# A schedule builder's clock learns of GpSimd's hold on VectorE's port: new order table, and batch 0's row copies by either engine

## The chip, the cores and the metric

The kernel runs on one core of one Trainium2 chip. The core has five engines with a queue each: TensorE (PE, with its weight loads PEld), VectorE (DVE), ScalarE (ACT), GpSimd (POOL) and SyncE (SP), which here only issues DMAs. Each engine takes its instructions in the order of the program. The metric is the device time of one execution in microseconds (us), as the median of several runs.

## The reference

Nystrom attention over 8 batches of 8 heads, 576 rows, 64 columns, and then a block with a layer norm and two dense layers:

```python
q_lm = q.reshape(B, H, 32, 18, D).mean(axis=3)       # 32 landmarks; k_lm likewise
A, Bm, C = sm(q, k_lm), sm(q_lm, k_lm), sm(q_lm, k)  # softmax(a @ b.T / 8)
Z = Bm.T / (norm1(Bm) * norminf(Bm) + 1e-06)
for _ in range(6):
    Z = 2 * Z - Z @ Bm @ Z
x = A @ Z @ C @ v                     # then heads side by side: 8 x 576 x 512
xn = (x - mu) / sqrt(var + 1e-06) * g_ln
out = x + maximum(xn @ w_ch1, 0) @ w_ch2             # 512 -> 2048 -> 512
```

## The kernel before

**Work.** Batches go through three stages. *Attention* (`attention0` for batch 0, `attention2` for the groups (1), (2), (3, 4), (5, 6), (7)): landmarks, the exponentials (`ec` of the k side, `ea` of the q side, by ScalarE's Exp out of the matmuls `psec` and `psea`), the softmax and six iterations of the 32 x 32 inverse (`st`; batch 2 and 7 do them as whole 128 x 128 matrices). The softmax of a batch is a chain on VectorE: `rsum`, `rcr`, `st`, `bmT`, a masked `st`, which TensorE then needs for the gram matrix. *First layer* (`first_layer`): hidden chunks `hT` of 128, each four matmuls into `psh` and a Relu. Since x itself is a product of `ea` and a small matrix, the layer multiplies the weights with the small matrix first (`m`). *Second layer* (`second_layer`): row blocks of 128, 16 matmuls `bank<-w,hT` each; from batch 4 on by seven products of half matrices (`seven_products`), for which VectorE mixes halves of `hT` and GpSimd those of `w2`. At its end VectorE adds x (`xblk`), scaled by `rstd`.

**Side work.** The rows of x (`xblk`) come from two matmuls per block of 128 rows (`rows_of`, `two_rows`, `part_of_rows`), copied out of PSUM. VectorE takes each block's statistics (`six`, `stats`: the MEASURE steps); when all of the batch `current[0]` are there, ScalarE makes `lnv` and `rstd` (`deviations`). The weights of the first layer are centered in place by VectorE in eight steps (`center_w1`, rows `w<-w,less`, two 128 x 512 pieces each). GpSimd casts the loaded q, k and v to fp16 (rows `nat<-stg`, `natv<-stg`; ScalarE may take a cast of q or k if GpSimd is behind); VectorE turns and adds them up for the landmarks (`xT`, `sT`, `part`: the JOB steps; a matmul and ScalarE's copy `lm` follow, the "spread").

**Order.** While the program is built, `run` draws the next piece from five streams, numbered 0 attention, 1 totals, 2 first layers, 3 rows of batch 0, 4 second layers, the first one that is ready by the builder's own clock (`Clock`), and between them `help_out` puts in side work, numbered 5 JOB, 6 MEASURE, 7 CENTER, 8 MIX, 9 MIX_W2, 10 CAST, 11 LOAD. `Clock.note` keeps, for every instruction noted, when its engine will be free (`free`) by a table of costs (`took`). The order of noting is the order in each engine's queue, and it is fixed once the program is built: the clock is not on the chip. MEASURE, CENTER and JOB are drawn only if

```python
if clock.free["DVE"] <= now + lead():     # 0.7 us once batch 1 is ready, 0.4 before
```

`sooner(n, at)` gives a copy to ScalarE (190 + 0.79 n ns by the builder's costs) or to VectorE (140 + 1.15 n), whichever it expects to be done first.

`AFTER` is a table of holds: `(0, 17): (4, 31)` says that stream 0 does not take its step of index 17 until stream 4 has taken 31 steps. In the kernel before, the second layer of batch 1 begins with step 53 of stream 4 (it sets `current[0]` to 1); attention step 20 (the 21st) is batch 2's first with `psec`. JOB steps 8 to 17 are batch 2's. The clock knows that a centering (`locks`) and a GpSimd instruction keep each other waiting when the GpSimd instruction has been noted already.

Of the kernel before, what the change touches and what calls it, by code (L numbers as in the profile page):

```python
# [16 lines left out]
P = 128  # L17
# [3 lines left out]
def kernel(  # L21
# [63 lines left out]
    class Clock:  # L85
# [74 lines left out]
        def note(self, i):  # L160
# [26 lines left out]
            if type(i).__name__ == "InstDMACopy":  # L187
                start = max(self.free[e], ready)
                self.free[e] = start + (580 if e == "SP" else 100)
                half_ = size[0][0] <= 64 and any(n.startswith("stg") for n in writes)  # L190
                self.wire = (max(start + 1650, self.wire)
                             + count[0] * size[0][0] * 4 / (150.0 if half_ else 385.0))
                self.loads = self.loads[-24:] + [(start, self.wire)]
                self.issued += 1
                late_ = 1500 if self.issued <= 4 else 600 + min(2200, 0.8 * (self.wire - start - 1650))
                done = self.wire + late_
                start = done
            elif e == "PE":
                cols = count[0]
                if self.count == self.mark - self.LEAD:  # L200
                    self.ahead = self.now()
                if self.count == self.mark:
                    self.mark += self.BLOCK
                    ready = max(ready, self.fetched)
                    asked = max(self.ahead, self.fetched - 200)
                    behind = max([w for t, w in self.loads if t <= asked] + [0.0])
                    self.fetched = max(asked + 1200, behind + 400) + 2450
                self.count += 1
                rows_, cols_ = tuple(i.tile_size)
                self.cells.append((self.now(), cols / 2.4 * rows_ * cols_ / 128 ** 2))  # L210
                if tuple(i.tile_size) == (128, 128):
                    if self.small:
                        self.free[e] = max(list(self.lanes.values()) + [self.free[e]]) + 100
                        self.small, self.lanes = False, {}
                    start = max(self.free[e], ready)
                    self.free[e] = start + max(cols / (1.2 if start < 5200 else 2.4) + 3, 56)
                    done = self.free[e] + 160
                else:
                    if not self.small:
                        self.small, self.lanes = True, {}  # L220
                        self.free[e] += 95
                    elif self.shape != (rows_, cols_):
                        self.free[e] = max(list(self.lanes.values()) + [self.free[e]]) + 85
                    self.shape = rows_, cols_
                    lane = [(a, c) for a in range(i.tile_position[0], i.tile_position[0] + rows_, 32)
                            for c in range(i.tile_position[1], i.tile_position[1] + cols_, 32)]
                    start = max([self.free[e], ready] + [self.lanes.get(x, 0.0) for x in lane])
                    self.lanes.update((x, start + max(cols / 2.4 + (19 if cols == 288 else 0), 30)) for x in lane)
                    self.free[e] = start + (8 if rows_ == 64 and cols < 128 else 4)
                    done = self.lanes[lane[0]] + 160  # L230
            else:
                start = max(self.free[e], ready)
                if e == "Pool":
                    for a, z in self.locks:
                        if a <= start < z:
                            start = z
                self.ready = start
                done = start + self.took(i, e, count[0], max(count[1:] + [0]))
                self.free[e] = done - self.OVERLAP[e]
                if e == "Pool":  # L240
                    self.pool = self.pool[-8:] + [(start, done)]
                if e == 'DVE' and count[0] == 1024 and writes[0] in parted_w1:
                    self.locks = self.locks[-4:] + [(start, done)]
            for n in reads:
# [620 lines left out]
                block_done(j)  # L865
        return copies

    def one_row(b):
        ea, zcbd = row_zc[b]
        j, at = row_blocks[b].pop(0)  # L870
        xb = x_of(j)
        psy = banks.take([P, 512])
        for u in range(U):
            MM(psy[:, ts(u, 4 * D)], ea[u][:, ds(at, P)], zcbd[u][:].rearrange("p h d -> p (h d)"))
        sooner(512, clock.at(psy))(xb[:], psy)
        block_done(j)

    def part_ready(b):
        return max(banks.next(2), 0.0 if row_part[b][0] in x_blk else xpool.next("xblk"))

# [11 lines left out]
    def rows_of(bs, ea, zcbd):  # L892
        for i, b in enumerate(bs):
            t0 = 0
            while t0 < S:
# [9 lines left out]
                for u in range(U):  # L905
                    MM(psy[:, ts(u, 4 * D)], ea[U * i + u][:, ds(at, P)],
                       zcbd[U * i + u][:].rearrange("p h d -> p (h d)"))
                (sooner(512, clock.at(psy)) if b else scalar.copy)(
                    xb[rows, :], psy[rows if n == P else ds(side, n), :])
                t0 += n  # L910
                if pb + n == P:
# [269 lines left out]
    def attention2(bs, c):  # L1181
# [152 lines left out]
                in1=heads_of[w % 2][:, :, None].broadcast_to([P, 4, D]),  # L1334
                op=ALU.mult)
        ready.update(bs)
        yield from (rows_later if bs[0] >= LATER else rows_of)(bs, ea, zcbd_buf[z0:z0 + W])

    stats_of, rstds = {}, {}

# [73 lines left out]
    class First:  # L1414
# [10 lines left out]
        def two_products_of_heads(self, f):  # L1425

            t = ps2.tile([P, 2, 512], FP32, name="psm", tag="p2")
            one = self.products(f, [banks.take([P, 512]), t[:, 0, :]])
            two = self.products(f + 1, [banks.take([P, 512]), t[:, 1, :]])
            copies = two_rows(self.b) if 2 * f in PAIRS and self.b >= LATER else lambda: None  # L1430
            self.copies(f, one)
            self.copies(f + 1, two)
            copies()
# [43 lines left out]
    def first_layer(b):  # L1477
# [3 lines left out]
            return  # L1481
        two = b >= 1
        if two:
            yield lambda: max(banks.next(2), ps2.next("p2", 2 if 0 in PAIRS and b >= LATER else 1), mprod.next("m16", 2), clock.at(l1.zt),
                              rows_ready(b) if 0 in PAIRS and b >= LATER else 0.0)
            l1.two_products_of_heads(0)
        else:
            yield lambda: max(banks.next(2), mprod.next("m16"), clock.at(l1.zt))
            l1.product_of_heads(0)
        for m in range(MCH):  # L1490
            yield lambda: max(ps2.next("p2"), clock.at(l1.m16[m // 4], *l1.ea),
                              part_ready(b) if m == PART[b % 2] and b in row_part else 0.0,
                              max(banks.next(2), xpool.next("xblk")) if m in ONES and b >= LATER else 0.0)
            l1.chunk(m)
            if m == PART[b % 2] and b in row_part:
                part_of_rows(b)
            if m in ONES and b >= LATER:
                one_row(b)
            if b in row_zc and not row_blocks[b] and b not in row_part:
                row_zc.pop(b)  # L1500
            chunks[b] = m + 1
# [3 lines left out]
                yield lambda: max(banks.next(2), mprod.next("m16"))  # L1505
                l1.product_of_heads(m // 4 + 1)
            if two and m == 4:
                yield lambda: max(banks.next(2), ps2.next("p2", 2 if 4 in PAIRS and b >= LATER else 1), mprod.next("m16", 2),
                                  rows_ready(b) if 4 in PAIRS and b >= LATER else 0.0)
                l1.two_products_of_heads(2)  # L1510
        for t in l1.ea:
            aexp.unpin(t)
        if b in (0, 1, 2, 4, 6, 7):
            asm.unpin(l1.zt)

    chunks, PART, PAIRS, ONES = {}, (8, 6), (0,4), ()
    LATER = 5

    def first_layer0(l1):
        l1.product_of_heads(0)  # L1520
# [239 lines left out]
    def help_out(hurry=False):  # L1760
# [66 lines left out]
    begun_first = [0]  # L1827

    AFTER = {
        (0, 17): (4, 31), (0, 23): (4, 75), (0, 34): (2, 51), (0, 53): (4, 171),  # L1830
        (0, 64): (4, 200), (0, 66): (2, 77), (0, 99): (4, 461), (0, 104): (4, 521),
        (0, 105): (4, 524), (0, 110): (4, 550), (1, 5): (4, 90), (2, 26): (0, 2),
        (2, 34): (4, 23), (2, 47): (4, 96), (2, 53): (4, 106), (2, 66): (4, 187),
        (2, 74): (4, 199), (2, 87): (4, 224), (2, 88): (4, 236), (2, 94): (4, 258),
        (2, 98): (4, 276), (2, 104): (4, 305), (2, 105): (4, 306), (2, 110): (4, 349),
        (2, 112): (4, 392), (2, 138): (4, 475), (2, 160): (4, 648), (3, 3): (2, 27),
        (4, 3): (0, 3), (4, 11): (2, 29), (4, 122): (0, 40), (4, 133): (0, 42), (4, 172): (0, 56),
        (4, 174): (0, 57), (4, 237): (2, 87), (4, 241): (2, 91), (4, 333): (2, 110),
        (4, 407): (2, 121), (4, 438): (2, 126), (4, 592): (2, 147), (4, 595): (2, 147),
        (4, 601): (2, 150), (4, 602): (2, 148), (4, 623): (2, 153), (5, 18): (4, 96),  # L1840
        (5, 26): (4, 119), (5, 30): (2, 66), (5, 43): (0, 53), (5, 49): (0, 65),
        (5, 62): (4, 265), (5, 64): (4, 281), (6, 5): (2, 43), (6, 15): (4, 208),
        (6, 34): (4, 640), (7, 5): (4, 88), (8, 1): (4, 290), (8, 7): (4, 559), (9, 4): (4, 231),
        (9, 9): (2, 93), (9, 14): (0, 80), (9, 15): (4, 257), (9, 16): (4, 279), (10, 5): (2, 46),
        (10, 10): (4, 71), (10, 20): (0, 43), (10, 30): (4, 196), (10, 34): (0, 84),
    }
    taken = [0] * 12
    JOB, MEASURE, CENTER, MIX, MIX_W2, CAST, LOAD = range(5, 12)
# [137 lines left out]
```

## Time and profile before

| | |
|---|---|
| runs | 263.0, 263.37, 263.76 us; median 263.37 us |
| profiled execution | 264.7 us, span 263.0 us, TensorE's clock granted in full |
| busy time | PE 252.0, DVE 209.7, ACT 171.5, POOL 137.3 us |
| HBM | 36.7 MB read, 9.4 MB written |

The span runs from the first instruction to the last. A row of the trace in order of time gives the start, the length, the engine, the line of the program (the helpers' lines L309 and L315 for nearly all), the operation, what it writes and reads by the program's names, shapes, how many were merged, and in brackets the idle time of the engine before it and what ended that. Rows of stretches give, for each engine, the busy time and in parentheses the number of instructions. A row of the waits gives who waited for whom: total us, times, longest.

### The profile page before, as it was taken

The page shows a single profiled execution, that of the slowest core. Times are in us where ns is not written, and L with a number is a line of the kernel's source. Part 1 is how long each engine was busy: PE and PEld are TensorE (multiplying, and loading weights), DVE is VectorE, ACT ScalarE, POOL GpSimd, SP SyncE. Part 2 cuts the span into 40 slices and gives each one's busy share as a digit, 9 for nine tenths or more (in the row PEclk, how much of TensorE's full clock was granted, in tenths as well). Part 3 has the DMA queues.
Part 4 walks back from the last instruction along what each step waited for, and adds up shares of the span by engine and source line. Part 5 has one row for each costly group of instructions (what it writes and reads, how often), then busy time and mean ns, then how long its engine had stood idle before and what let it go on. Part 6 is the DMA issues. An engine that isn't in the chain of part 4 may idle for free.

```text
span 263.0 us, 8556 instructions
## 1 busy us (share of the span) xinstructions
PE 252.0 (96%) x3519; PEld 167.8 (64%) x3519; DVE 209.7 (80%) x475; ACT 171.5 (65%) x335; POOL 137.3 (52%) x163
## 2 busy tenths in 40 slices
PE   7799889999799999999999999999999999999994
PEld 6645654556355574456655556688877875888883
DVE  2677774999979998989898967788389899696862
ACT  2588797548675887678987767655877854775000
POOL 5287779999962869989999938300000005000000
PEclk9999999999999999999999999999999999999999
DMA  6999999999957898779813011110240006100705
GB/s 241 377 396 377 378 392 386 354 267 318 358 159 207 234 374 294 191 185 298 270 53 82 7 40 40 42 40 4 53 109 2 4 16 156 32 2 0 161 16 185
DMA packets 24126, 46.68 MB, mean 178 GB/s; under 512 B 2964, under 2 KB 3224, under 8 KB 24088
## 3 DMA queue, kind: packets, MB, share of 16 engines
q1 hardware_dynamic: 23608, 45.50, 54.5%
q10 hardware_dynamic: 480, 0.66, 0.7%
q8 instruction: 27, 0.44, 0.7%
q14 instruction: 11, 0.09, 0.1%
HBM read 36.70 MB, written 9.44 MB: 175 GB/s over the span
## 4 chain that ended last, share of the span: by engine, by line
PE 75%; DVE 10%; DMA 8%; ACT 3%; issue 1%; POOL 1%; SPq 0%; ACTq 0%; DVEq 0%
PE bank L315 49%; PE psh L315 19%; DMA wstg<-in_moe_w_ch_dram 6%; DVE m L309 2%; DMA stg<-in_k_dram 2%; DVE w L309 2%; PE pscv L315 2%; PE psd L315 2%; ACT xblk L309 1%; DVE six L309 1%; PE psea L315 1%; DVE xblk L309 1%; DVE part L309 1%; ACT hT L309 1%; PE psec L315 1%
## 5 line engine op out<-in xcount | busy, mean ns | idle before, releaser
L315 PE MATMUL bank<-w,hT 128*128 128x512 f16 (+3 forms) x528 | 110.0, 335 | 0.0
L309 ACT ACTIVATE hT<-psh 128x576 f16<-128x576 f32 x122 | 75.9, 653 | 22.5 <-PE psh L315 21.1
L315 PEld LDWEIGHTS <-hT 128*128 128x128 f16 x656 | 60.2, 98 | 30.5 <-issue 5.0
L315 PE MATMUL psh<-ea,m 128*128 128x288 f16 x512 | 78.5, 286 | 1.0 <-ACT ec L309 0.9
L315 PEld LDWEIGHTS <-m 128*128 128x128 f16 x512 | 49.4, 98 | 19.7 <-issue 2.3
L309 DVE SCALAR_TENSOR_TENSOR xblk<-bank,rstd,xblk 128x256 f32<-128x256 f32 (+2 forms) x77 | 39.1, 542 | 15.6 <-PE bank L315 15.3
L309 POOL TENSOR_TENSOR ea<-ea,lns 128x576 f16<-128x576 f16 x14 | 18.0, 1298 | 54.0 <-ACT lns L309 54.0
L309 POOL CAST nat<-stg 128x1152 f16<-128x1152 f32 x24 | 28.9, 1223 | 9.8 <-DMA stg<-in_v_dram 4.7
L309 DVE BATCH_NORM_STATS2 six<-xblk 128x6 f32<-128x512 f32 x36 | 24.3, 675 | 2.1 <-ACT xblk L309 1.9
L309 POOL CAST natv<-stg 128x1152 f16<-128x1152 f32 (+1 forms) x17 | 19.3, 1161 | 7.8 <-DMA stg<-in_v_dram 7.8
L309 DVE STREAM_TRANSPOSE xT<-nat 128x576 uint32<-128x576 uint32 x28 | 21.4, 762 | 0.0
L309 DVE SCALAR_TENSOR_TENSOR st<-st,bank 128x128 f16<-128x128 f16 (+3 forms) x36 | 13.2, 365 | 6.6 <-PE bank L315 6.4
L315 PE MATMUL bank<-w2mix 128*128 128x256 f16 x128 | 17.3, 273 | 0.0
L315 PE MATMUL bank<-w2mix,hT 128*128 128x256 f16 x128 | 16.9, 273 | 0.0
L309 ACT COPY xblk<-bank 128x512 f32<-128x512 f32 (+1 forms) x21 | 12.4, 594 | 5.9 <-PE bank L315 5.8
L309 ACT ACTIVATE lns<-psd 128x576 f32<-128x576 f32 x16 | 10.3, 643 | 7.9 <-PE psd L315 7.6
L309 DVE TENSOR_REDUCE part<-xT 128x32 f16<-128x576 f16 x20 | 14.4, 741 | 0.2
L315 PEld LDWEIGHTS <-st 32*32 32x32 f16 (+1 forms) x380 | 7.0, 90 | 11.3 <-DVE st L309 6.2
L315 PEld LDWEIGHTS <-w2mix 128*128 128x128 f16 x128 | 12.4, 98 | 1.9
L309 ACT ACTIVATE ec<-psec 128x256 f16<-128x256 f32 (+1 forms) x42 | 11.9, 424 | 2.3 <-PE psec L315 2.0
L309 POOL TENSOR_TENSOR asum<-asum 128x256 f32<-128x256 f32 (+1 forms) x20 | 12.4, 621 | 1.6
L309 ACT CAST m<-bank 128x512 f16<-128x512 f32 x16 | 9.3, 589 | 5.8 <-PE bank L315 5.8
(133 smaller groups left out, 374.4 us busy)
## 6 DMA issues: line engine op xcount, KB each, us to landing
stg<-in_q_dram SPq DMA_DIRECT2D x16, 576.0 KB, 6.4
stg<-in_k_dram SPq DMA_DIRECT2D x16, 576.0 KB, 5.9
out_dram<-xblk SPq DMA_DIRECT2D x66, 128.0 KB, 2.4
wstg<-in_moe_w_ch_dram SPq DMA_DIRECT2D x16, 512.0 KB, 7.3
stg<-in_v_dram SPq DMA_DIRECT2D x5, 576.0 KB, 7.6
stg<-in_v_dram SPq DMA_DIRECT2D x40, 72.0 KB, 2.7
stg<-in_v_dram SPq DMA_DIRECT2D x6, 288.0 KB, 4.9
stg<-in_v_dram SPq DMA_DIRECT2D x12, 144.0 KB, 2.9
```

The source lines that it names most:

```text
L309: return lambda *args, **kw: keep(getattr(self.engine, op)(*args, **kw))
L315: keep(nc.tensor.matmul(o, l, r, start=start, stop=stop, tile_position=(rb, cb), skip_group_check=(skip or cb != 0)))
```

## The change

One line in `Clock.note`: when a GpSimd instruction is noted that starts before one of the last two centerings and ends after that one's start, VectorE's free time is put off by the overlap. `rows_of` copies batch 0's rows by `sooner`, as those of other batches, in place of ScalarE always. `PAIRS` names the batches (5, 6, 7) for which `two_rows` is used, in place of `LATER`; `one_row`, which no batch used, goes; the rows of a group's batches are drawn batch by batch. `AFTER` has 46 entries in place of 67; 23 keys stand in both, 9 of them with the same value.

```diff
--- before.py
+++ after.py
@@ -239,6 +239,7 @@
                 self.free[e] = done - self.OVERLAP[e]
                 if e == "Pool":
                     self.pool = self.pool[-8:] + [(start, done)]
+                    self.free["DVE"] += sum(done - a for a, _ in self.locks[-2:] if start < a < done)
                 if e == 'DVE' and count[0] == 1024 and writes[0] in parted_w1:
                     self.locks = self.locks[-4:] + [(start, done)]
             for n in reads:
@@ -865,16 +866,6 @@
                 block_done(j)
         return copies
 
-    def one_row(b):
-        ea, zcbd = row_zc[b]
-        j, at = row_blocks[b].pop(0)
-        xb = x_of(j)
-        psy = banks.take([P, 512])
-        for u in range(U):
-            MM(psy[:, ts(u, 4 * D)], ea[u][:, ds(at, P)], zcbd[u][:].rearrange("p h d -> p (h d)"))
-        sooner(512, clock.at(psy))(xb[:], psy)
-        block_done(j)
-
     def part_ready(b):
         return max(banks.next(2), 0.0 if row_part[b][0] in x_blk else xpool.next("xblk"))
 
@@ -905,7 +896,7 @@
                 for u in range(U):
                     MM(psy[:, ts(u, 4 * D)], ea[U * i + u][:, ds(at, P)],
                        zcbd[U * i + u][:].rearrange("p h d -> p (h d)"))
-                (sooner(512, clock.at(psy)) if b else scalar.copy)(
+                sooner(512, clock.at(psy))(
                     xb[rows, :], psy[rows if n == P else ds(side, n), :])
                 t0 += n
                 if pb + n == P:
@@ -1334,7 +1325,9 @@
                 in1=heads_of[w % 2][:, :, None].broadcast_to([P, 4, D]),
                 op=ALU.mult)
         ready.update(bs)
-        yield from (rows_later if bs[0] >= LATER else rows_of)(bs, ea, zcbd_buf[z0:z0 + W])
+        for i, b in enumerate(bs):
+            two = slice(U * i, U * i + U)
+            yield from (rows_later if b in PAIRS else rows_of)((b,), ea[two], zcbd_buf[z0:z0 + W][two])
 
     stats_of, rstds = {}, {}
 
@@ -1427,7 +1420,7 @@
             t = ps2.tile([P, 2, 512], FP32, name="psm", tag="p2")
             one = self.products(f, [banks.take([P, 512]), t[:, 0, :]])
             two = self.products(f + 1, [banks.take([P, 512]), t[:, 1, :]])
-            copies = two_rows(self.b) if 2 * f in PAIRS and self.b >= LATER else lambda: None
+            copies = two_rows(self.b) if 2 * f in PAIRS.get(self.b, ()) else lambda: None
             self.copies(f, one)
             self.copies(f + 1, two)
             copies()
@@ -1481,21 +1474,18 @@
             return
         two = b >= 1
         if two:
-            yield lambda: max(banks.next(2), ps2.next("p2", 2 if 0 in PAIRS and b >= LATER else 1), mprod.next("m16", 2), clock.at(l1.zt),
-                              rows_ready(b) if 0 in PAIRS and b >= LATER else 0.0)
+            yield lambda: max(banks.next(2), ps2.next("p2", 2 if 0 in PAIRS.get(b, ()) else 1), mprod.next("m16", 2), clock.at(l1.zt),
+                              rows_ready(b) if 0 in PAIRS.get(b, ()) else 0.0)
             l1.two_products_of_heads(0)
         else:
             yield lambda: max(banks.next(2), mprod.next("m16"), clock.at(l1.zt))
             l1.product_of_heads(0)
         for m in range(MCH):
             yield lambda: max(ps2.next("p2"), clock.at(l1.m16[m // 4], *l1.ea),
-                              part_ready(b) if m == PART[b % 2] and b in row_part else 0.0,
-                              max(banks.next(2), xpool.next("xblk")) if m in ONES and b >= LATER else 0.0)
+                              part_ready(b) if m == PART[b % 2] and b in row_part else 0.0)
             l1.chunk(m)
             if m == PART[b % 2] and b in row_part:
                 part_of_rows(b)
-            if m in ONES and b >= LATER:
-                one_row(b)
             if b in row_zc and not row_blocks[b] and b not in row_part:
                 row_zc.pop(b)
             chunks[b] = m + 1
@@ -1505,16 +1495,15 @@
                 yield lambda: max(banks.next(2), mprod.next("m16"))
                 l1.product_of_heads(m // 4 + 1)
             if two and m == 4:
-                yield lambda: max(banks.next(2), ps2.next("p2", 2 if 4 in PAIRS and b >= LATER else 1), mprod.next("m16", 2),
-                                  rows_ready(b) if 4 in PAIRS and b >= LATER else 0.0)
+                yield lambda: max(banks.next(2), ps2.next("p2", 2 if 4 in PAIRS.get(b, ()) else 1), mprod.next("m16", 2),
+                                  rows_ready(b) if 4 in PAIRS.get(b, ()) else 0.0)
                 l1.two_products_of_heads(2)
         for t in l1.ea:
             aexp.unpin(t)
         if b in (0, 1, 2, 4, 6, 7):
             asm.unpin(l1.zt)
 
-    chunks, PART, PAIRS, ONES = {}, (8, 6), (0,4), ()
-    LATER = 5
+    chunks, PART, PAIRS = {}, (8, 6), {b: (0, 4) for b in (5, 6, 7)}
 
     def first_layer0(l1):
         l1.product_of_heads(0)
@@ -1827,22 +1816,17 @@
     begun_first = [0]
 
     AFTER = {
-        (0, 17): (4, 31), (0, 23): (4, 75), (0, 34): (2, 51), (0, 53): (4, 171),
-        (0, 64): (4, 200), (0, 66): (2, 77), (0, 99): (4, 461), (0, 104): (4, 521),
-        (0, 105): (4, 524), (0, 110): (4, 550), (1, 5): (4, 90), (2, 26): (0, 2),
-        (2, 34): (4, 23), (2, 47): (4, 96), (2, 53): (4, 106), (2, 66): (4, 187),
-        (2, 74): (4, 199), (2, 87): (4, 224), (2, 88): (4, 236), (2, 94): (4, 258),
-        (2, 98): (4, 276), (2, 104): (4, 305), (2, 105): (4, 306), (2, 110): (4, 349),
-        (2, 112): (4, 392), (2, 138): (4, 475), (2, 160): (4, 648), (3, 3): (2, 27),
-        (4, 3): (0, 3), (4, 11): (2, 29), (4, 122): (0, 40), (4, 133): (0, 42), (4, 172): (0, 56),
-        (4, 174): (0, 57), (4, 237): (2, 87), (4, 241): (2, 91), (4, 333): (2, 110),
-        (4, 407): (2, 121), (4, 438): (2, 126), (4, 592): (2, 147), (4, 595): (2, 147),
-        (4, 601): (2, 150), (4, 602): (2, 148), (4, 623): (2, 153), (5, 18): (4, 96),
-        (5, 26): (4, 119), (5, 30): (2, 66), (5, 43): (0, 53), (5, 49): (0, 65),
-        (5, 62): (4, 265), (5, 64): (4, 281), (6, 5): (2, 43), (6, 15): (4, 208),
-        (6, 34): (4, 640), (7, 5): (4, 88), (8, 1): (4, 290), (8, 7): (4, 559), (9, 4): (4, 231),
-        (9, 9): (2, 93), (9, 14): (0, 80), (9, 15): (4, 257), (9, 16): (4, 279), (10, 5): (2, 46),
-        (10, 10): (4, 71), (10, 20): (0, 43), (10, 30): (4, 196), (10, 34): (0, 84),
+        (0, 17): (4, 31), (0, 34): (2, 51), (0, 64): (4, 200), (0, 99): (4, 488),
+        (0, 105): (4, 522), (1, 5): (4, 89), (2, 26): (0, 2), (2, 74): (4, 196),
+        (2, 80): (4, 205), (2, 88): (4, 237), (2, 94): (4, 257), (2, 98): (4, 277),
+        (2, 107): (4, 329), (2, 110): (4, 349), (2, 112): (4, 392), (2, 113): (4, 393),
+        (2, 133): (4, 471), (2, 152): (4, 631), (2, 157): (4, 640), (3, 3): (4, 4),
+        (4, 3): (0, 3), (4, 53): (0, 21), (4, 133): (0, 42), (4, 173): (0, 57),
+        (4, 438): (2, 126), (4, 452): (2, 131), (4, 511): (0, 101), (4, 615): (2, 150),
+        (5, 12): (4, 34), (5, 15): (2, 42), (5, 18): (0, 34), (5, 43): (4, 172), (5, 49): (0, 66),
+        (5, 50): (0, 68), (5, 61): (4, 261), (6, 15): (4, 203), (6, 16): (2, 85),
+        (6, 21): (0, 71), (6, 25): (4, 390), (6, 29): (2, 134), (6, 35): (4, 641), (7, 5): (1, 6),
+        (9, 7): (4, 238), (10, 1): (2, 31), (10, 8): (4, 55), (10, 20): (4, 132),
     }
     taken = [0] * 12
     JOB, MEASURE, CENTER, MIX, MIX_W2, CAST, LOAD = range(5, 12)
```

## The prediction

> **What bounds the kernel now.** I read the page's first part, the busy time by stretch, then the waits of the one bad stretch and its engines in order of time. The page:
>
> ```profile
> PE 252.0 (96%) x3519; PEld 167.8 (64%) x3519; DVE 209.7 (80%) x475; ACT 171.5 (65%) x335; POOL 137.3 (52%) x163
> ```
>
> Stretches (length, then busy time of PE, PEld, DVE, ACT, POOL, clock, DMA):
>
> ```profile
> 45.00:65.00 20.00, 19.89 (x172) 11.30 (x170) 18.90 (x32) 12.09 (x23) 19.37 (x20) 1.00 1.00 318
> 65.00:75.00 10.00, 8.51 (x153) 4.26 (x152) 9.66 (x25) 7.01 (x17) 9.35 (x11) 1.00 0.91 306
> 75.00:240.00 165.00, 164.88 (x2374) 110.10 (x2373) 138.24 (x309) 119.80 (x236) 77.42 (x77) 1.00 0.39 112
> ```
>
> TensorE is the bound: from 75 to 240 us it idles 165 - 164.88 = 0.12 us. Only its idle time can be won, 263.0 - 252.0 = 11.0 us, most of it at the start (loads) and the last stores, which the diff does not touch. Between lie 1.49 us in 65 to 75 and about 0.9 us near 36. The waits of 64 to 76 us:
>
> ```profile
> PE bank L315 <- DVE st L309: 1.5, 2, 0.9
> ...
> ACT lnv L309 <- DVE stats L309: 0.8, 1, 0.8
> ```
>
> and, in order of time, VectorE (start, length, what), then ScalarE, then TensorE:
>
> ```profile
> 62.78 2.90 DVE L309 TENSOR_TENSOR w<-w,less 128x1024 f16<-128x1024 f16 x2
> ...
> 68.80 0.66 DVE L309 TENSOR_TENSOR w<-w,less 128x1024 f16<-128x1024 f16 x1
> 69.38 0.75 DVE L309 SCALAR_TENSOR_TENSOR xblk<-bank,rstd,xblk 128x512 f32<-128x512 f32 x1
> 70.04 0.21 DVE L309 TENSOR_REDUCE rsum<-bank 128x2 f32<-128x64 f32 x1
> ```
>
> ```profile
> 65.86 1.19 ACT L309 ACTIVATE hT<-psh 128x576 f16<-128x576 f32 x2 [0.25 <-PE psh L315]
> 66.94 1.15 ACT L309 CAST nat<-stg 128x1152 f16<-128x1152 f32 x1
> 68.92 0.30 ACT L309 ACTIVATE lnv<-stats,eps_ln 128x5 f32<-128x5 f32 x1 [0.83 <-DVE stats L309]
> 69.25 0.21 ACT L309 ACTIVATE rstd<-lnv 128x5 f32<-128x5 f32 x1
> 69.36 0.21 ACT L309 ACTIVATE bank<-bank 128x64 f32<-128x64 f32 x1
> ```
>
> ```profile
> 66.15 1.24 PE L315 MATMUL bank<-w,hT 128*128 128x512 f16 x5
> ...
> 70.77 0.19 PE L315 MATMUL bank<-st,bones 128*128 128x64 f16 x1 [0.60 <-DVE st L309]
> 71.85 0.28 PE L315 MATMUL bank<-st 128*128 128x128 f16 x2 [0.89 <-DVE st L309]
> ```
>
> Batch 2's attention starts its softmax here. Its first matmuls are done at 67.5, but its Exp waits until 69.36 behind batch 1's lnv, which waits for VectorE; `rsum` comes at 70.04, and TensorE idles 0.60 + 0.89 us for `st`. VectorE is late because the two centerings at 62.78 took 1.35 and 1.63 us, where the last three take 0.68: GpSimd was casting.
>
> **Clock.** A GpSimd step that is noted after a centering, but lies before it in time, now pushes VectorE's free time. Following the builder through the kernel before, the condition holds once: the cast of v noted after the 46th first-layer step would add 0.85 + 0.24 = 1.09 us, for the two centerings that run at 62.78. No instruction is added. The builder takes a statistics or centering step only while VectorE is free within 0.7 us, so those noted just then come later: the centering at 68.80 falls behind the softmax, and `rsum` comes 0.58 us earlier (69.38 - 68.80).
>
> **Table.** 23 of its 46 keys were there before (9 entries unchanged), 23 are new. Most move a step past one to eight matmuls of 0.22 us. I cost those at nothing between 75 and 240 us: TensorE is never empty, so one stream's matmuls take the other's place, 0.12 us could be won, and lost cover costs one VectorE round trip, 0.6 to 0.9 us by the two waits above. In the last 20 us the h mixes end at 246.0 and their first reader starts at 247.08; `s2` itself is done at 244.1, 3 us of cover, so the two late holds there cost nothing.
>
> One entry matters: second-layer step 53, where batch 1's second layer begins, is held until attention's 21st step, the matmuls `psec` at 67.3. Before, it ran ahead of them. It sets `current` to 1, without which batch 1's lnv and rstd are not issued: these now come behind the Exp. The cast of index 8 is held until 55 second-layer steps are taken, so the one after it, ScalarE's of 1.15 us at 66.94, falls behind too. Three of the five matmuls at 66.15 belong to batch 1 and move behind `psec`: 3 x 0.22 = 0.65 us. Queued behind the held step is all second-layer work; the first layer has none either, since batch 1's is finished and batch 2's needs this softmax. So TensorE would reach `psec` at 67.33 - 0.65 = 66.68, but its buffers come free only when ScalarE's hT ends, 65.86 + 1.19 = 67.05: about 0.4 us idle. After it, the old 1.49 us shrinks by the 0.65 us of matmuls and the 0.58 us of the earlier chain, to 0.26. Sum: 0.4 + 0.26 - 1.49 = **-0.83 us**; bounds -1.49 (all gone) and 0 (only moved).
>
> The first jobs hold back VectorE work of batch 2: step 12 to second-layer step 34 (an add at 55.09), step 15 to first-layer step 42 (four operations from 60.39 to 62.05). Held until about 62.3, the latter end near 64.0. The spread matmul and ScalarE's `lm` copy follow (before, done at 63.10, 1.05 us behind the sums), so by 65.1; `psec` is due at 67.05: 2.0 us of cover. If it is gone, every further microsecond is idle TensorE.
>
> **Batch 0's copies.** ScalarE copies a row block in 0.58, VectorE in about 0.7 (its 128x512 `xblk` rows take 0.74), and the builder takes whichever is done first. The first, third and fourth stay. The second, at 35.15, waited for ScalarE's hT while VectorE idled 1.56 us: it moves. ScalarE's Exp at 35.62 then waits for its matmul alone (it ended at 35.38): 0.2 us earlier, and with it the `ec` tiles whose end TensorE awaits at 36.93. **-0.2 us**; bounds 0 (the `psec` matmuls end at 36.0 anyway) and -0.5 (the whole copy). The fifth, at 42.14, also moves, into VectorE's gap after 41.28, costing the next `st` 0.1 us at most. The rest (`PAIRS`, `one_row`, `rows_of` per batch) leaves the same instructions.
>
> **A rule against it.** Centerings beside a cast took 1.41, 1.35 and 1.63 us; the first ended 0.55 us after the cast that was running, the third also. The one at 73.29 started ahead of a cast and took 0.68, and that cast took 1.61 instead of 1.14. The Trainium skill, SBUF — State Buffer, "Who interferes with whom", says that the shared port is an exclusive lock held for a whole instruction, by whoever came first. The trace agrees. By that rule a better clock wins nothing on VectorE itself while GpSimd casts without pause. I take 0 for this too, since GpSimd is busy 19.37 of 20 us up to 65; were all three blocked centerings to fall after 75, VectorE would gain 4.39 - 3 x 0.68 = 2.35 us, but TensorE no more than its 1.49.
>
> **The sum.** -0.83 - 0.2 = -1.03 us. The profiled execution took 264.7 us (span 263.0, 1.7 around it): 263.7, span 262.0. It is 1.3 above the median of 263.37, against which I forecast **262.3**.
>
> **Rivals.**
> (1) The wait only moves: TensorE idles ahead of `psec` what it idled behind it, because the four statistics at 65.61 to 68.88 still precede `rsum`. For it: VectorE has no gap from 47 to 75. Against: the matmuls now behind `psec` are fresh cover. 263.37 - 0.2 = 263.2.
> (2) Slower, by the held jobs. If VectorE runs the two blocked centerings (2.98 us) and two statistics (0.79 each) ahead of them, they end at 64.0 + 4.6 = 68.6, `lm` at 69.6, and TensorE, with both layers empty, idles from 66.7 to 69.6: 2.9 us in place of 1.49, so +1.4, **264.8**. It decides once the last of batch 2's sums ends after 67.1 (before: 62.05), where that idle stretch passes the old one. For it: VectorE is full, and what is held there loses its place. Against: the builder prefers batch 2's jobs as soon as they may run.
> (3) The edit does nothing for the stall, the push comes at another step, and two of the small holds each cost a round trip while none pays: 263.37 + 0.6 + 0.9 = 264.9. The order before is tight at many of the dropped entries (the step stood exactly at its limit), so they were holding something back.
>
> **Chances.** Forecast 0.50; rival 1 0.20; rival 2 0.18; rival 3 0.12. A measurement of this kernel tells about 0.3% (0.8 us) from no change. The forecast lies on the faster side of it, rival 1 within, 2 and 3 beyond: 0.50, 0.20, 0.30. The range goes from both lower bounds (263.37 - 1.49 - 0.5 = 261.4; 261.2 with the 0.12 us that the middle could give) to rival 3's 264.9.
>
> **What would show it.** Right: lnv and rstd behind batch 2's Exp; `rsum` before 69.5; TensorE's two waits for `st` near 70 under 0.5 us together; a short wait ahead of `psec`; the second row copy on VectorE; 75 to 240 still without idle time. Wrong: TensorE idle over 1 us ahead of `psec` with `lm` late (rival 2), the old waits still there at 70 (1), or new waits past 75 us (3).

## The result

The kernel became slower: 264.98 us median (264.74 to 266.9, 13 runs) against 263.67 us (262.85 to 264.42, 13 runs), a ratio of 1.0064 with an interval of 1.0044 to 1.0084. The ratio is of the means. The profiled execution took 264.93 us, span 263.2. The forecast was 262.3. Three of the 13 runs (266.17, 266.54, 266.9) have a mean TensorE clock of 0.991 to 0.993, the other ten 0.997 or more; the last section says what that costs. Without the three the means still stand at a ratio of 1.005, 1.33 us. Runs over 1.5% above the fastest of the same kernel, three of e11's eight, are left out of the ratios below.

The page and the stretches of the kernel after, columns as before:

```profile
PE 252.6 (96%) x3519; PEld 168.5 (64%) x3519; DVE 211.8 (80%) x477; ACT 172.5 (66%) x334; POOL 136.2 (52%) x162
```

```profile
45.00:65.00 20.00, 20.00 (x181) 11.52 (x174) 19.10 (x38) 12.66 (x23) 19.17 (x20) 1.00 0.99 316
65.00:75.00 10.00, 7.78 (x148) 3.85 (x146) 9.22 (x20) 6.83 (x17) 7.74 (x10) 1.00 0.91 298
75.00:240.00 165.00, 164.94 (x2373) 109.90 (x2371) 138.77 (x308) 120.76 (x236) 78.22 (x77) 1.00 0.39 113
```

Of these three only 65 to 75 has lost: TensorE is busy for 7.78 us where the trace of before showed 8.51. The waits of 64 to 76 us name what the prediction wanted to remove, now larger:

```profile
PE bank L316 <- DVE st L310: 2.2, 2, 1.3
```

ScalarE, TensorE, VectorE and GpSimd of the kernel after in order of time:

```profile
66.40 0.21 ACT L310 ACTIVATE bank<-bank 128x64 f32<-128x64 f32 x1 [0.23 <-ACT hT L310]
...
68.35 0.35 ACT L310 ACTIVATE lnv<-stats,eps_ln 128x5 f32<-128x5 f32 x1
```

```profile
66.12 0.79 PE L316 MATMUL psec<-xT,lm 32*32 32x288 f16 x32
66.84 2.55 PE L316 MATMUL bank<-w,hT 128*128 128x512 f16 x11
70.72 0.19 PE L316 MATMUL bank<-st,bones 128*128 128x64 f16 x1 [1.33 <-DVE st L310]
71.80 0.29 PE L316 MATMUL bank<-st 128*128 128x128 f16 x2 [0.89 <-DVE st L310]
```

```profile
65.26 4.16 DVE L310 TENSOR_TENSOR w<-w,less 128x1024 f16<-128x1024 f16 x3
69.34 0.74 DVE L310 SCALAR_TENSOR_TENSOR xblk<-bank,rstd,xblk 128x512 f32<-128x512 f32 x1
70.00 0.21 DVE L310 TENSOR_REDUCE rsum<-bank 128x2 f32<-128x64 f32 x1
...
70.98 0.76 DVE L310 TENSOR_TENSOR st<-bmT,mask 128x256 f16<-128x256 f16 x1
```

```profile
62.85 3.32 POOL L310 CAST nat<-stg 128x1152 f16<-128x1152 f32 x3
66.26 1.48 POOL L310 TENSOR_TENSOR asum<-nat 128x512 f32<-128x512 f16 x1
67.81 1.92 POOL L310 TENSOR_TENSOR asum<-asum 128x256 f32<-128x256 f32 x2
```

ScalarE's Exp is at 66.40 (69.36 before) and lnv stands behind it, as forecast. VectorE takes up that result only at 70.00: three centerings stand ahead of `rsum`, 1.39 us each beside GpSimd's casts and sums.

The profiled execution of before was a long one (264.7). A second profile of the unchanged kernel, 263.3 us and near the median, is the better one to compare with. Its VectorE and TensorE:

```profile
61.63 2.89 DVE L309 TENSOR_TENSOR w<-w,less 128x1024 f16<-128x1024 f16 x2
...
67.64 0.77 DVE L309 TENSOR_TENSOR w<-w,less 128x1024 f16<-128x1024 f16 x1
...
68.99 0.21 DVE L309 TENSOR_REDUCE rsum<-bank 128x2 f32<-128x64 f32 x1
...
69.97 0.43 DVE L309 TENSOR_TENSOR st<-bmT,mask 128x256 f16<-128x256 f16 x1
```

```profile
69.71 0.19 PE L315 MATMUL bank<-st,bones 128*128 128x64 f16 x1 [0.26 <-DVE st L309]
70.46 0.29 PE L315 MATMUL bank<-st 128*128 128x128 f16 x2 [0.56 <-DVE st L309]
```

TensorE's wait there is 0.26 + 0.56 = 0.82 us, not 1.49, so after is 1.40 us worse in this wait, nearly the whole difference of the spans (263.2 - 261.6).

### The profile page after: what moved, and what is told of

The parts are those of the page before. It is cut to its first block, busy times and chain, and to the rows that moved or that the text cites. A ratio compares the mean times of both kernels' runs of the same rounds, so it can differ in the third digit from the quotient of the medians.

```text
span 263.2 us, 8553 instructions
## 1 busy us (share of the span) xinstructions
PE 252.6 (96%) x3519; PEld 168.5 (64%) x3519; DVE 211.8 (80%) x477; ACT 172.5 (66%) x334; POOL 136.2 (52%) x162
## 4 chain that ended last, share of the span: by engine, by line
PE 81%; DVE 12%; DMA 3%; ACT 2%; issue 1%; SPq 1%; DVEq 0%
PE bank L316 53%; PE psh L316 21%; DMA stg<-in_k_dram 3%; DVE m L310 2%; DVE w L310 2%; PE psd L316 2%; PE pscv L316 2%; DVE xblk L310 1%; DVE six L310 1%; PE psea L316 1%; DVE part L310 1%; DVE xT L310 1%; PE psec L316 1%; PE psr L316 1%; DVE st L310 1%
## 5 line engine op out<-in xcount | busy, mean ns | idle before, releaser
L310 ACT ACTIVATE hT<-psh 128x576 f16<-128x576 f32 x124 | 77.5, 653 | 22.5 <-PE psh L316 20.9
L310 POOL CAST nat<-stg 128x1152 f16<-128x1152 f32 x23 | 26.5, 1166 | 12.0 <-DMA stg<-in_v_dram 6.0
L316 PE MATMUL bank<-w2mix,hT 128*128 128x256 f16 x128 | 17.5, 273 | 0.0
L310 ACT COPY xblk<-bank 128x512 f32<-128x512 f32 (+1 forms) x16 | 9.3, 591 | 6.4 <-PE bank L316 6.4
L310 ACT ACTIVATE ea<-psea 128x576 f16<-128x576 f32 x14 | 8.3, 648 | 7.0 <-PE psea L316 7.0
```

The source lines that it names most:

```text
L310: return lambda *args, **kw: keep(getattr(self.engine, op)(*args, **kw))
L316: keep(nc.tensor.matmul(o, l, r, start=start, stop=stop, tile_position=(rb, cb), skip_group_check=(skip or cb != 0)))
```

## The experiments

All were timed in five rounds against the kernel before. "Order kept" means that apart from the moved or added instructions every queue is as in its parent; the others were drawn anew by the builder. In the expectations up to e4, A, B and C are the theories that the one of e1 states; V is the theory that the loss is VectorE's queue ahead of batch 2's softmax; from e9 on B is the one that is worked out behind e6. The diffs are shown shortened.

| run | ratio to before, interval |
|---|---|
| e1 before again | 1.001 (0.9996 to 1.0023) |
| e2 after, rows on ScalarE, order kept | 1.0142 (1.0124 to 1.016) |
| e3 before, rows on VectorE, order kept | 1.006 (1.0045 to 1.0075) |
| e4 after without the clock's line | 1.0083 (1.0056 to 1.011) |
| e5 after, centerings later, order kept | 1.0065 (1.004 to 1.0091) |
| e6 before, centerings later, order kept | 1.0008 (0.9989 to 1.0028) |
| e7 before, new table | 1.0209 (1.0186 to 1.0232) |
| e8 after, old table | 1.0208 (1.0184 to 1.0232) |
| e9 after, one centering less, order kept | 1.0009 (0.9996 to 1.0021) |
| e10 before, two centerings later, order kept | 1.0009 (0.9992 to 1.0026) |
| e11 before, two operations more at 61 us, order kept | 1.0075 (1.0039 to 1.011) |
| e12 before, two operations more at 89 us, order kept | 1.005 (1.0032 to 1.0068) |

**e1, the kernel before unchanged.**

> The kernel before, unchanged, for a second profile of it: the profiled execution shown so far took 264.7 us, 1.0 more than the median of its 13 runs (263.67), and TensorE waited 1.18 us at 27.8 for a late cast of k. Theory A (the loss lies between 26 and 46 us: VectorE's copies of batch 0's rows hold up batch 1's inverse, so that the changed kernel throws away a start that the kernel before usually keeps): ratio 1.00, a span near 262, without the wait at 27.8, and batch 1's zt copy on VectorE near 45.2 (45.96 in the first profile, 45.88 in the changed kernel). Theory B (the loss lies between 46 and 79 us, in VectorE's order ahead of batch 2's softmax): zt near 45.9 as in both profiles, and rsum of batch 2 near 69 instead of 70.0. Theory C (the loss comes after 79 us): equal up to the first chunk of batch 2's first layer (83.6 us in both), and about 1 us less after that.

263.42 us (262.92 to 264.63, 12 runs); its profile is the second one above. No theory is met in full: the `zt` copy came at 45.51, between A's 45.2 and B's 45.9, and TensorE still waited 0.62 us near 27.8; `rsum` came at 68.99, as B has it; and the kernel was 1.37 us ahead of after before 80 us, against C. One kernel's executions differ by over 1 us, and the first profile of before, at the upper end, oversold the stall.

**e2 and e3, the copies.** In after's order, issued on ScalarE; in before's, the second, fourth and fifth on VectorE:

```diff
-                sooner(512, clock.at(psy))(xb[rows, :], ...)
+                # noted as planned; where sooner() took VectorE:
+                nc.scalar.copy(xb[rows, :], ...)

-                (sooner(512, clock.at(psy)) if b else scalar.copy)(xb[rows, :], ...)
+                # e3: noted as planned; for batch 0's t0 of 128, 384, 512:
+                nc.vector.tensor_copy(out=xb[rows, :], in_=...)
```

> The changed kernel's own order on every engine, but the three row copies of batch 0 that it put on VectorE (34.05, 38.58 and 41.66 us) are issued by ScalarE at the same place in the order. Theory A: batch 1's first st after its gram comes about 0.6 us earlier (40.13 in the changed kernel), zt near 45.2, and the ratio falls from 1.0064 to between 1.002 and 1.004. Theory B and C: the ratio stays within 0.001 of 1.0064.

> The kernel before with its own order, but the second, fourth and fifth row copies of batch 0 issued by VectorE in place of ScalarE. Theory A: 0.6 to 1.0 us slower, ratio 1.002 to 1.004, with batch 1's zt later by as much. Theory B and C: ratio 0.999 to 1.001.

e2 took 267.04 us and e3 265.02. e2 refutes the 1.002 to 1.004 expected of theory A: in after's order the copies are worse on ScalarE (batch 1's `pszt` comes 1.1 us later than in after; TensorE's clock dropped as well, in all five runs by their means, last section). In before's order they are worse on VectorE. So neither engine is the better one as such. e3 fits no theory: A wants batch 1's `pszt` later by the whole loss, B and C want no loss. Batch 1 reaches `pszt` only 0.09 us later than in e1, yet the first centering met a cast (e3, then e1):

```profile
48.64 0.74 DVE L312 SCALAR_TENSOR_TENSOR m<-less,zsum,psm 128x512 f16<-128x512 f16 x1
49.30 1.44 DVE L312 TENSOR_TENSOR w<-w,less 128x1024 f16<-128x1024 f16 x1
```

```profile
49.21 0.69 DVE L309 TENSOR_TENSOR w<-w,less 128x1024 f16<-128x1024 f16 x1
```

In e1 it started 0.13 us before GpSimd's first cast ended (48.20 to 49.34); in e3 it started 0.26 us into the second (49.04 to 50.19) and ended 0.54 us behind that. A shift of 0.33 us against the casts, 0.09 of the centering and 0.24 of the casts, decided 0.75 us. Some 0.3 us of e3's loss lies outside the span: time less span is 2.0 to 2.1 us in its runs, 1.9 to 2.0 in those of e11 and e12, and 1.7 to 1.8 in all others. Why stays open.

**e4, without the clock's line.**

```diff
-                    self.free["DVE"] += sum(done - a for a, _ in self.locks[-2:] if start < a < done)
```

> The changed kernel without the new line in the clock (table and row copies as changed). Only a few instructions change places then. All theories here: ratio within 0.002 of 1.0064, so the line itself carries none of the loss. If the three centerings in a row at 65.26 us come from it (theory B), rsum of batch 2 comes earlier than 70.0 and the ratio falls by 0.002 or more.

265.67 us: no faster than after, so the line carries none of the loss. (Three runs with a mean clock of 0.997 or more took 264.82 to 265.08, as after's do; the other three, at 0.992 to 0.994, 266.26 to 266.77.) Followed through the builder, its condition holds once in the changed program, for 0.47 us, when batch 2's softmax has been noted already. The profiled execution of e4 was slowed by TensorE's clock (last section).

**e5 and e6, the centerings behind the softmax**, in after and in before:

```diff
     def center_w1(f, c):
...
-        dve.tensor_tensor(out=o, in0=o, in1=less, op=ALU.add)
+        clock.note(...)                  # planned where it was
+        put_off[LATE[i]].append((o, less))   # issued behind the gram matrix's st, iterations 1 and 2
```

> The changed kernel; only on VectorE, the three centerings that stood ahead of batch 2's softmax (4.16 us from 65.26) are issued later: behind the st of the gram matrix, behind iteration 1 and behind iteration 2. Every other queue is the same, instruction by instruction. Theory V (the loss is VectorE's queue ahead of the softmax): xblk at about 66.2 (its matmuls end at 66.07), rsum at about 66.9 in place of 70.00, the masked st done by 68.5, so that TensorE reaches its two matmuls on st at 69.4 with no wait: its 2.22 us of idle time there go. 264.98 - 2.2 = 262.8, a ratio of 0.996 to 0.999 to the kernel before. Rival (the work only moves: VectorE is over 90% busy from 45 to 75 us, so what is put off delays the iterations by as much): rsum early all the same, but new idle time of TensorE between 71 and 80 of 1 to 2 us, and a ratio of 1.003 or more.

> The kernel before with the same edit: its three centerings of 61.6 to 68.4 (2.89 and 0.77 us) behind the gram matrix's st, iteration 1 and iteration 2; every other queue is unchanged. Theory V: the statistics end 2.9 us earlier, lnv then comes right behind ScalarE's cast at 67.3, the Exp at about 67.8, rsum at about 68.1 in place of 68.99, and TensorE's idle time of 0.82 us falls to 0.1: ratio 0.996 to 0.998. Rival (it only moves): 1.000 or more, with the idle time at 72 to 80.

e5 took 265.06 us, e6 263.91: nothing gained, and the rival is right in both. In e6 TensorE's one wait left there is of 0.79 us, at 75.65. VectorE and TensorE of e5:

```profile
67.09 0.21 DVE L310 TENSOR_REDUCE rsum<-bank 128x2 f32<-128x64 f32 x1
...
70.68 1.46 DVE L1432 TENSOR_TENSOR w<-w,less 128x1024 f16<-128x1024 f16 x1
72.06 1.22 DVE L310 TENSOR_TENSOR w<-w,less 128x1024 f16<-128x1024 f16 x1
...
74.32 1.57 DVE L1432 TENSOR_TENSOR w<-w,less 128x1024 f16<-128x1024 f16 x1
...
76.86 0.93 DVE L1432 TENSOR_TENSOR w<-w,less 128x1024 f16<-128x1024 f16 x1
```

```profile
69.53 0.19 PE L316 MATMUL bank<-st,bones 128*128 128x64 f16 x1
69.56 0.28 PE L316 MATMUL bank<-st 128*128 128x128 f16 x2
...
74.07 0.42 PE L316 MATMUL psd<-ea,bones 128*128 128x288 f16 x2 [0.56 <-DVE cv L310]
...
77.00 0.31 PE L316 MATMUL bank<-st 128*128 128x160 f16 x2 [1.36 <-DVE st L310]
```

`rsum` came 2.9 us earlier and both old waits are gone, exactly as wanted. But the centerings now stand between the iterations, again beside GpSimd (L1432 are the moved ones), and TensorE waits 0.56 + 1.36 = 1.92 us there. So the wait shows where the shortage appears, and is not its cause.

**What the traces add up to.** Between batch 1's `pszt` and batch 2's `pszt` VectorE runs the same list of operations in nearly every kernel, order apart (e7 and e8 have an eighth centering and one or two operations more in it, e11 its two additions). Times in us; the centerings' time runs from the start of each to the start of the next operation, and a gap over 0.1 us counts as idle. Batch 2's `pszt` in after and in e1:

```profile
81.16 0.24 PE L316 MATMUL pszt<-st,cv 32*32 32x32 f16 x16
```

```profile
79.79 0.23 PE L315 MATMUL pszt<-st,cv 32*32 32x32 f16 x16
```

| trace | batch 1's pszt | batch 2's pszt | between | centerings | VectorE idle | end of span | end less pszt |
|---|---|---|---|---|---|---|---|
| before, first | 45.61 | 81.18 | 35.57 | 6.53 | 1.94 | 262.96 | 181.78 |
| e1 before again | 45.16 | 79.79 | 34.63 | 6.10 | 1.82 | 261.59 | 181.80 |
| after | 45.53 | 81.16 | 35.63 | 6.68 | 2.01 | 263.21 | 182.05 |
| e3 | 45.25 | 80.86 | 35.61 | 6.57 | 1.94 | 262.93 | 182.07 |
| e5 | 45.84 | 81.57 | 35.73 | 7.00 | 1.91 | 263.63 | 182.06 |
| e6 | 44.94 | 79.96 | 35.01 | 5.39 | 2.80 | 261.72 | 181.76 |
| e9 (6 centerings) | 45.81 | 80.35 | 34.54 | 6.12 | 1.81 | 262.43 | 182.08 |
| e10 | 44.99 | 79.85 | 34.86 | 5.69 | 2.49 | 261.64 | 181.79 |

In these eight the last column takes two values, 181.8 and 182.1 (e4 and e11 give them too, 182.07 and 181.78; e2 gives 182.36): in them the time is all but settled when batch 2 reaches `pszt`. e7, e8 and e12 lose later as well (185.3, 185.0, 182.9). The time between is VectorE's list, 32.2 to 33.9 us of work, and 1.8 to 2.8 us of idle time. So theory B, which e9, e11 and e12 test: from 45 to 81 us VectorE is the bound, and TensorE's idle time shows only where the order lets the lack of work appear. After against e1: 0.37 us from batch 1's `pszt`, 1.00 from the list (centerings 0.58, the masked `st` 0.34, idle 0.19, the rest -0.11), 0.25 behind it: 1.62 of 263.21 - 261.59. e12, whose order up to 81 us is that of before, repeats e1's sum (34.63 between, 6.11 for the centerings, 1.82 idle). Batch 1's `pszt` lies between 44.94 and 45.61 in the six traces with before's order up to there, and between 45.49 and 45.84 in the four with after's.

**e7 and e8, the table and the code apart.** The kernel before with the new `AFTER`; the kernel after with the old:

```diff
-    AFTER = { ... }     # e7: before's 67 entries; e8: after's 46
+    AFTER = { ... }     # e7: after's 46; e8: before's 67
```

> The kernel before with the new table of holds alone; the row copies stay with ScalarE and the clock's line is not there. The builder draws a new order from it. If the copies on VectorE carry the loss (they cost a ratio of 1.006 by themselves in the order of before): 1.000 to 1.002, with psec of batch 2 near 66 and TensorE's idle time at 66 to 73 under 1.2 us. If the table carries it by putting batch 2's centerings ahead of the softmax: 1.003 to 1.006, rsum no earlier than 69.5, idle time near 2 us.

> The changed kernel with the old table of holds: the copies by either engine and the clock's line stay. If the copies carry the loss: 1.004 to 1.007, with the first centering near 49.3 beside a cast (1.4 us in place of 0.7) and rsum of batch 2 near 69.7. If the table carries it: 0.999 to 1.002, TensorE's idle time at 66 to 73 at 0.8 us as before.

269.24 and 269.13 us: both expectations fail, far on the slow side. Either half alone costs over three times what both cost together. The likely reason, which no run tests by itself, is that the steps a table counts are those of the order it was made for. In e7 TensorE loses 3.7 us in a stretch that was full before:

```profile
100.00:150.00 50.00, 46.28 (x775) 25.43 (x773) 42.40 (x94) 37.22 (x80) 45.58 (x51) 1.00 0.69 216
```

So the change's cost cannot be shared out among its parts by leaving one out.

**e9, one centering left out.**

```diff
+        if i == 2:
+            clock.note(...)              # planned, not issued
```

> The changed kernel with one centering left out, the second of the three ahead of batch 2's softmax (that part of the first layer's weights stays uncentered); nothing else differs in any queue. Theory B (from batch 1's zt to batch 2's zt, 45 to 81 us, VectorE is the bound: it runs the same list of operations in every kernel, and the end comes 178.1 to 178.4 us after batch 2's pszt): pszt 1.35 to 1.4 us earlier, near 79.8, and the end as much: about 263.6, a ratio of 0.999 to 1.001. Rival (something else takes over, ScalarE or the casts): less than 0.5 us gained, a ratio above 1.003.

263.97 us by the median, 1.0 below after: nearly three quarters of the 1.35 to 1.4 expected and well above the rival's 0.5. The ratio of 1.0009 is within the forecast, helped by the clock: all 12 runs have it at 0.998 or more. VectorE's work is what costs, though the remaining six centerings took 6.12 us, 1.02 each in place of 0.95. (The 178.1 to 178.4 us of the expectation run to TensorE's last matmul, the table's last column to the end of the span.)

**e10, two centerings later, to fill the gap of e6.**

```diff
-    LATE = {1: gram, 2: iteration 1, 3: iteration 2}     # e6
+    LATE = {1: gram, 2: iteration 1}
```

> The kernel before with only the two centerings of 61.6 to 64.5 put off, behind the gram matrix's st and behind iteration 1; the third stays, and fills the gap of 1.14 us in which VectorE waited for ScalarE's Exp when all three were put off. Theory B: VectorE's sum for centerings as in the run with all three late (5.39 us in place of 6.10) and its idle time as before (1.8 in place of 2.8): batch 2's pszt at about 79.1 in place of 79.8, 0.6 us won, a ratio of 0.997 to 0.999. Rival (put off, they meet GpSimd's casts again, or an iteration waits): 1.000 or more.

263.53 us, no gain: the rival is right. The centerings' sum fell by 0.41 us and VectorE's idle time rose by 0.67. No version here beats the kernel before.

**e11 and e12, two statistics operations more on VectorE.**

```diff
+        for _ in range(2 if j == 4 else 0):      # e12: j == 11
+            nc.vector.bn_stats(out=six[:], in_=x_blk[j][:])
         dve.bn_stats(out=six[:], in_=x_blk[j][:])
```

> The kernel before with one row block's statistics operation on VectorE issued three times in place of once at 60.8 us (the same result each time), 2 x 0.66 = 1.3 us more work between the two zt. Theory B: batch 2's pszt and the end 1.3 us later, a ratio of 1.004 to 1.006. Rival (TensorE is the bound, and VectorE has slack that TensorE's other work covers): 1.000 to 1.002.

> The same two additional operations, at a row block of batch 2 (near 86 to 89 us), behind batch 2's zt. Theory B: nothing waits for VectorE there, the ratio is 0.999 to 1.001. Rival (VectorE, 90% busy from 75 to 150 us, bounds there too): 1.004 to 1.006.

e11's five runs counted took 264.46 to 267.25 us. In the profiled one, of 267.16, batch 2's `pszt` came at 83.43 and TensorE's clock was halved meanwhile, so the ratio of 1.0075 is no clean measure of the two operations. The two runs with a mean clock of 0.999 (the others have 0.991 to 0.994) took 264.46 and 264.48, 0.9 above the 263.59 of before: more than the rival's 1.002, less than B's 1.004. e12 took 264.68, the end 0.95 us later than in e1, and here theory B's limit at 81 us fails. Batch 2's `pszt` did not move (79.66), but the sums for batches 3 and 4 came late, and TensorE waited (e12, then e1):

```profile
95.69 0.38 PE L315 MATMUL bank<-part,spread 128*128 128x256 f16 x2 [0.93 <-DVE part L309]
```

```profile
94.73 0.38 PE L315 MATMUL bank<-part,spread 128*128 128x256 f16 x2
```

VectorE's sum still binds at 96 us, where e1 has no such wait and so gives no sign of it.

## Why the prediction was wrong, step by step

- **The bound.** This failed. "TensorE is the bound: only its idle time can be won" reads a full TensorE as the limit. From 45 to 81 us, and to 96 by e12, VectorE's list sets when the next work arrives. The row that said so was shown and read past: VectorE 18.90 of 20 and 9.66 of 10 us busy.
- **The hold on (4, 53).** Right in its mechanism: `psec` at 66.12, Exp at 66.40, lnv and ScalarE's cast behind it. The 0.4 us of idle time ahead of `psec` did not come.
- **The term of -0.83.** Wrong in sign. `rsum` was to come 0.58 us earlier because the clock would put a centering behind the softmax, and TensorE's 1.49 us of waiting to shrink to 0.26. The line fired too late for that, the new order put three centerings ahead, `rsum` came at 70.00 where the typical execution of before has 68.99, and the waiting was 2.22 us. Even e5, where `rsum` came at 67.09, gained nothing.
- **The start of the sum.** The 1.49 us came from an execution 1.3 us above the median of the three runs then known, 1.0 above that of all 13. A typical one shows 0.82 us.
- **The copies, -0.2.** Wrong in sign too. The second and fifth moved as forecast; the fourth, which was to stay, moved as well. The Exp behind the second came 0.38 us earlier than in e1 (34.78 and 35.16), but TensorE's wait near 36 us went from 0.92 to 1.03, now for VectorE's `st`, and the early start was lost in VectorE's queue:

```profile
34.05 0.69 DVE L310 COPY xblk<-bank 128x512 f32<-128x512 f32 x1 [0.56 <-PE bank L316]
...
38.58 0.69 DVE L310 COPY xblk<-bank 128x512 f32<-128x512 f32 x1 [0.53 <-PE bank L316]
39.30 0.69 DVE L310 BATCH_NORM_STATS2 six<-xblk 128x6 f32<-128x512 f32 x1
40.03 0.18 DVE L310 BATCH_NORM_AGGREGATE stats<-six 128x2 f32<-128x6 f32 x1
40.13 0.25 DVE L310 SCALAR_TENSOR_TENSOR st<-st,bank 128x128 f16<-128x128 f16 x1
```

  Batch 1's `rsum` is at 35.60 (36.16 in e1), but its first iteration's `st` stands at 40.13 (39.17) behind the fourth copy and its statistics: +0.37 us at `pszt`.
- **Collisions, 0.** Mis-sized: 0.58 us for the centerings and 0.34 for the masked `st`. The Trainium skill, SBUF — State Buffer, "Who interferes with whom", has an operation of VectorE with two inputs in SBUF contend with GpSimd's reads, and whoever came first hold the pair for a whole instruction. The traces agree on both sides: centerings of 0.66 to 0.69 us took up to 1.57 in e5, and GpSimd's sum at 66.26 took 1.48 where free ones of its shape take 1.16. These sizes are not after's alone: the first trace of before has 6.53 us for the centerings and the same 0.76 for the masked `st`.
- **The other holds.** Right: from 75 to 240 us TensorE idles 0.06 us, batch 2's sums end at 63.74 (forecast 64.0), `lm` at 65.06 (65.1). One reading was off by 0.1 us (the row of the h mixes, 244.82 + 1.28, ends at 246.10, not 246.0), and nothing hangs on it.
- **Rivals.** The first, that the wait only moves, had the right argument (VectorE has no gap from 47 to 75) and its sign came, the old waits still there at 70. But it looked for the idle time ahead of `psec`, where none came, and its 263.2 was 1.8 us short because it priced the move at nothing. The second and third came near the time, 264.8 and 264.9, by other ways: no sum ended after 67.1, and no new wait came past 75 us.

How much of the 1.00 us in VectorE's list is after's order and how much is chance in the profiled execution stays open: the two executions of before differ by 0.94 us in the same sum. The profiled execution of after is a typical one (ten of the 13 runs took 264.74 to 265.5), e1 and e12 agree, and the medians differ by 1.31 us where these spans differ by 1.62; so chance may hold some 0.3 us of it, an estimate from these numbers. What is not chance is that none of after's 13 runs was under 264.74. Which part of the change puts the order so stays open as well, since the parts could not be told apart.

## What to carry to other kernels

An idle stretch of the full engine is where a shortage appears, not what causes it: sum the queue of the engine that feeds it between two fixed points, and if work and idle time together hardly change with the order, reordering moves the wait and wins nothing. Before costing a stall at its size in one profile, look at a second execution of the same kernel. A table of step counts is best taken as part of the order it was made for: here the planner changed without it, or the table alone, cost over three times what both cost together.

## What was not expected of the hardware

TensorE's granted clock fell to 0.50 for 3.41 us in the profiled executions of e2 (from 74.12), e4 (71.48) and e11 (72.90), each just after TensorE had been idle for 1.04 + 0.99, 1.05 + 0.99 and 1.71 + 0.89 us with one matmul between. In e4 five matmuls took 2.31 us that take 1.25 in e1; the stretch of the drop, with the clock in the last column but two:

```profile
70.00:75.00 5.00, 3.61 (x52) 1.13 (x55) 3.82 (x10) 2.23 (x3) 3.15 (x4) 0.66 0.78 225
```

The profiled execution of after, with 1.33 + 0.89 us, more than e2 and e4 have, has no such drop at that place. The Trainium skill, TensorE: Matmul & The Clock Gate, "Part 1: The HAM clock gate (the "warmup" mystery)", gives a free-running window of 3413 ns after which an idle array is halved. The traces agree on the window: in each of them the times between the clock's changes, from the first full grant to the last drop, are whole multiples of 3.413 us (in e4 full for 64.85 us, 19 of them, then half for one), and these windows lie elsewhere in each execution. They differ on the idleness: the array was not idle for a whole window. Cut by each trace's own windows, the one that ends at the drop has 1.81 us of idle time in e2, 1.93 in e4 and 2.60 in e11. After's waits fell into two windows, 1.74 and 0.48 us. After, then e4, each in the window with the most:

```profile
67.91:71.32 3.41, 1.67 (x8) 0.58 (x6) 3.27 (x8) 2.04 (x6) 3.17 (x4) 1.00 1.04 389
```

```profile
68.07:71.48 3.41, 1.48 (x7) 0.49 (x5) 3.27 (x9) 1.85 (x6) 2.55 (x4) 1.00 1.06 362
```

So the same idle time costs or does not cost, depending on where the window lies, and here the border is near 1.8 us, just over half a window (one with 1.86 us, among the last matmuls of before's first trace, kept its clock). It makes a stall of 2 us a worse risk than its length: some 1.3 us more in e4 (266.26 us, where its runs with a full clock took 264.82 to 265.08). After's three runs with a mean clock of 0.991 to 0.993, like that of e4's profiled one (0.994), took 1.2 to 1.9 us more than its median; they were not profiled, so it is likely and not shown that each had such a drop.
